# Attention: the second query chunk's probabilities are transposed by TensorE too, in a third filling of one PSUM bank

## The chip, the cores and the metric

The program runs on one core of one Trainium2 chip. The metric is the device time of one execution, in microseconds (us). Names of engines: PE is TensorE (PEld its weight loads), DVE is VectorE, ACT is ScalarE, POOL is GpSimd, and SP is the queue of SyncE, from which most DMAs are issued.

## The reference, cut to what matters

Causal attention over 4 batches and 12 heads of 448 tokens of 64 numbers, then two mixture-of-experts layers with top-1 routing (1792 tokens, 768 numbers, 8 experts, 1024 hidden numbers). The change touches the attention alone.

```python
scores = scale * np.matmul(q, k.transpose(0, 1, 3, 2))
scores = np.where(mask, -1000000000.0, scores)      # mask: above the diagonal
scores = scores - np.max(scores, axis=-1, keepdims=True)
attn = np.exp(scores)
attn = attn / (np.sum(attn, axis=-1, keepdims=True) + 1e-09)
out = np.matmul(attn, v)
...
x = _moe_ref(x=x, **moe_kwargs)
return _moe2_ref(x=x, **moe2_kwargs)
```

## The kernel before

**Tiling.** Two heads make a pair (index e is 0 or 1), 24 pairs in all. The 448 queries of a head are 4 chunks of 112 (c is 0 to 3). Chunk c sees c + 1 blocks of 112 keys, so a head has 1 + 2 + 3 + 4 = 10 blocks of 112x112 probabilities. They lie in one tile `ex` in SBUF, chunk by chunk: `boff` (L392) gives the first block of each chunk, [0, 1, 3, 6].

**A loop of stages.** One pass of the loop over g works on four pairs at once: scores and exponentials of pair g, the transposed probabilities of t = g - 1, the product with the values of v = g - 2, and routing work for r = g - 3. Each engine runs its instructions in the order in which the program was written.

- `qk` (L395): PE writes the mask and the scores of two chunks for both heads into four PSUM banks. `rowmax` (L410): DVE finds each row's extreme. `expo` (L415): ACT writes the exponentials to `ex`. Chunks 0 and 1 come first, chunks 2 and 3 later in the pass; there are four banks, so the next scores wait for the exponentials before.
- The product with the values needs the probabilities with keys in the partitions, so each block is transposed, as a high half and a low half in f16. **By DMA:** chunks 0, 1 and 2 (ND = 6 blocks a head): `halves_hi` (L424) lets ACT write `ah`, one instruction a head, and `halves_lo` (L429) lets DVE write `al` = `ex` - `ah`, one a head; `transposed` (L420) issues a DMA transpose from SP for each, into `th` and `tl`. **By PE:** chunk 3 (4 blocks): `last_chunk` (L436) has PE transpose the four blocks of one head into the left 448 columns of one PSUM bank, `tb[0]`; ACT then writes the high half `ph`, and DVE the low half `pl`. This is one filling of the bank; there are two in a pass, one for each head (`late[0]` and `late[1]`).
- `values` (L449): for each block five small matmuls into `av` (and, for the last group of columns, into the right part of `tb[1]`, called the tail). `combine` (L479): DVE divides by the row sums and writes `xb`.
- `route_t` (L495): PE transposes 128 columns of `xb` into the left of `tb[1]`; ACT and DVE split them into `xTh` and `xTl`; `route_l` (L508) multiplies them with the router's weights.
- Once a batch is done, its routing (a few dozen tiny DVE instructions, some PE work, a few POOL instructions and DMAs) is spread over three passes: `tick` takes one step of it after many of the big DVE instructions. Its PE work writes the right part of `tb[0]` (`side`, L338), and only the step that `tick(True)` takes, right after the first `qk` of a pass, may start that PE work.
- `scale_pair` and `split_v` on POOL prepare later pairs.

**SP in a pass:** DMA transposes of `ah` from the pass before, loads for four pairs ahead, DMA transposes of `al`, stores of `xb`. From pass 18 on, one weight load too.

After the attention the two expert layers follow, on PE almost without a gap.

Of the kernel before, what the change touches and what calls it, by code (L numbers as in the profile page):

```python
# [9 lines left out]
F32 = mybir.dt.float32  # L10
F32R = mybir.dt.float32r
BF16 = mybir.dt.bfloat16
F16 = mybir.dt.float16
# [43 lines left out]
def attention_two_moe_kernel(  # L57
# [243 lines left out]
    def drain(gen):  # L301
        for _ in gen:
            pass
# [12 lines left out]
    NB = NCH * (NCH + 1) // 2  # L316
    ND = NB - NCH
    exs = [at_p.tile([CP, 2, NB, CP], F32, name=f"ex{i}") for i in range(NEX)]
# [4 lines left out]
    phs = [av_p.tile([CP, 2 * NCH * CP + 16], F16, name=f"ph{i}") for i in range(NTP)]  # L323
    pls = [av_p.tile([CP, 2 * NCH * CP + 16], F16, name=f"pl{i}") for i in range(NTP)]
    for t in ahs + als:
        vec.memset(t[:, :, :, CP:], 0.0)
# [5 lines left out]
    for t in phs + pls:  # L332
        vec.memset(t[:, 2 * NCH * CP :], 0.0)


    tb = [ps_t.tile([P, 512], F32, tag="t", name="tb0"), ps_x.tile([P, 512], F32, tag="t2", name="tb1")]

    def side():  # L338

        return tb[0][:, S:] if tb else ps_t.tile([P, 512], F32, tag="t", name="t")  # L340

# [49 lines left out]

    boff = [0, 1, 3, 6]  # L392
    scs, nms, avs = {}, {}, {}
# [30 lines left out]
    def halves_hi(g):  # L424
        for e in range(2):
            act.activation(ahs[g % NAH][:, e, :, :CP], exs[g % NEX][:, e, :ND], AF.Copy, scale=ASC)
            transposed(ths[g % NTH], ahs[g % NAH], e)
# [7 lines left out]

    def last_chunk(g, e):  # L436

        pt = tb[0][:CP, :S]
        for j in range(NCH):
            pe.transpose(pt[:, j * CP : (j + 1) * CP], exs[g % NEX][:, e, ND + j], ident[:CP, :CP])  # L440
        yield
        ph, pl = (t[g % NTP][:, e * S : (e + 1) * S] for t in (phs, pls))
        act.activation(ph, pt, AF.Copy, scale=ASC)
        yield
        vec.scalar_tensor_tensor(out=pl, in0=pt, scalar=ASC, in1=ph, op0=ALU.mult, op1=ALU.subtract)
        tick()

    VW = HD + 1

    def values(g, e):  # L450

        if e == 1 and g not in tails:
            tails[g] = tb[1][:, S:]
        if e == 0:
            avs[g] = ps_x.tile([P, 512], F32, tag="av", name=f"av{g}")
        v0, v1, v2 = (t[:, e] for t in vss[g])
        for c in range(NCH):
            k = c if e == 0 else NCH + (c - 1) % NCH
            at = k * VW
            for j in range(c + 1):  # L460
                if c < NCH - 1:
                    o = (e * ND + boff[c] + j) * CP
                    hi, lo = (t[g % NTH][:CP, o : o + P] for t in (ths, tls))
                else:
                    o = (e * NCH + j) * CP
                    hi, lo = (t[g % NTP][:, o : o + P] for t in (phs, pls))
# [316 lines left out]
    for g in range(NPR + 3):  # L783
# [12 lines left out]
        if 0 <= v < NPR and v % PB == 0:  # L796
            xbs[v // PB] = xb_p.tile([CP, NCH, D], F32, tag="xb", name=f"xb{v // PB}")
        late = [last_chunk(t, e) if 0 <= t < NPR else iter(()) for e in range(2)]
        if g < NPR:
            qk(g, (0, 1))  # L800
        tick(True)
        if g < NPR:
            for c in range(2):
                both(rowmax, g, c)
                if g == c == 0:
                    both(expo, 0, 0, ticks=False)
                    scale_pair(1, vec)
            for c in range(g == 0, 2):
                both(expo, g, c, ticks=False)
        next(late[0], None)  # L810
        next(late[0], None)
        if 0 <= t < NPR:
            halves_lo(t, (0,))
        next(late[0], None)
        if 0 <= t < NPR:
# [16 lines left out]
        if 0 <= v < NPR:  # L832
            values(v, 0)
        if PB <= r < NPR and r % PB < NCH:
# [8 lines left out]
        if g < NPR:  # L843
            qk(g, (2, 3))
            for c in range(2, NCH):
                both(rowmax, g, c)
        next(late[1], None)
        for c in range(2, NCH):
            if g < NPR:
                both(expo, g, c, ticks=False)  # L850
            next(late[1], None)
        if 0 <= v < NPR:
            values(v, 1)
        if 0 <= r < NPR:
            route_l(r)
        if 0 <= v < NPR:
            combine(v, xbs[v // PB])
        if g < NPR:
            halves_hi(g)
        if g + 2 < NPR:  # L860
            scale_pair(g + 2, pool)
        if g == 0:
# [656 lines left out]
```

## Time and profile before

| what | us |
|---|---|
| median of 3 runs | 905.91 (905.5 to 911.83) |
| the profiled execution | 908.99 |
| its span, first to last instruction | 907.3 |
| PE busy | 848.7 (94%) |
| DVE busy | 678.2 (75%) |
| ACT busy | 427.1 (47%) |
| POOL busy | 399.0 (44%) |

A busy time counts the time in which at least one instruction of the engine is on record. PE's matmuls overlap and their ends are modelled, so the starts of its instructions say more than their lengths. A wait "A <- B" is idle time of A that ended when B did; "issue" is idle time for which the profile shows no reason. The clock of PE is either 2.4 GHz (1.00 in the columns) or 1.2 GHz (0.50).

### The profile page before, as it was taken

The page shows a single profiled execution, that of the slowest core. Times are in us where ns is not written, and L with a number is a line of the kernel's source. Part 1 is how long each engine was busy: PE and PEld are TensorE (multiplying, and loading weights), DVE is VectorE, ACT ScalarE, POOL GpSimd, SP SyncE. Part 2 cuts the span into 40 slices and gives each one's busy share as a digit, 9 for nine tenths or more (in the row PEclk, how much of TensorE's full clock was granted, in tenths as well). Part 3 has the DMA queues.
Part 4 walks back from the last instruction along what each step waited for, and adds up shares of the span by engine and source line. Part 5 has one row for each costly group of instructions (what it writes and reads, how often), then busy time and mean ns, then how long its engine had stood idle before and what let it go on. Part 6 is the DMA issues. An engine that isn't in the chain of part 4 may idle for free. (4 is left out here: it accounts for less than half of the span.)

```text
span 907.3 us, 20634 instructions
## 1 busy us (share of the span) xinstructions
PE 848.7 (94%) x6818; PEld 729.4 (80%) x6818; DVE 678.2 (75%) x1782; ACT 427.1 (47%) x777; POOL 399.0 (44%) x433
## 2 busy tenths in 40 slices
PE   5999999988788999999999999999999999999985
PEld 2677776766576899988899989888898898998984
DVE  6888998987876766787747964468786778976783
ACT  4667867775435754575535552245112133221323
POOL 6224245423266264544542564432654544545530
PEclk8899999998799999999999999999999999999997
DMA  7799998998737774687515761120291133511110
GB/s 227 143 160 164 206 199 178 206 174 169 238 97 262 280 260 163 210 290 257 185 46 172 239 229 62 49 73 6 62 328 56 54 108 117 182 43 59 49 38 16
DMA packets 114451, 137.39 MB, mean 151 GB/s; under 512 B 78381, under 2 KB 82787, under 8 KB 114288
## 3 DMA queue, kind: packets, MB, share of 16 engines
q1 hardware_dynamic: 101376, 108.76, 44.4%
q0 software_dynamic: 12912, 26.83, 9.3%
q8 instruction: 57, 0.93, 0.4%
q14 instruction: 106, 0.87, 0.3%
HBM read 101.48 MB, written 19.92 MB: 134 GB/s over the span
## 5 line engine op out<-in xcount | busy, mean ns | idle before, releaser
L748 POOL DMA_INDIRECT xg<-x,xi x128 | 134.4, 1050 | 101.2 <-DMA x<-yb,mg 47.7
L956 PE MATMUL h<-w1h,xh 128*128 128x512 f32 x408 | 164.6, 403 | 2.4 <-issue 1.4
L958 PE MATMUL h<-w1h,xl 128*128 128x512 f32 x408 | 161.1, 395 | 0.9 <-DVE xl L941 0.9
L957 PE MATMUL h<-w1l,xh 128*128 128x512 f32 x408 | 161.2, 395 | 0.7 <-DVE w1l L698 0.7
L1021 PE MATMUL o<-w2h,hh 128*128 128x384 f32 x528 | 137.5, 341 | 0.2 <-issue 0.2
L1021 PE MATMUL o<-w2h,hl 128*128 128x384 f32 x528 | 135.3, 337 | 0.5 <-DVE hl L971 0.5
L1021 PE MATMUL o<-w2l,hh 128*128 128x384 f32 x528 | 134.4, 336 | 0.0
L998 DVE STREAM_TRANSPOSE hs<-h 32x256 f32<-32x256 f32 x240 | 107.1, 446 | 14.3 <-PE h L958 8.5
L418 ACT ACTIVATE ex<-sc,nm 112x112 f32<-112x112 f32 (+1 forms) x192 | 82.8, 499 | 60.9 <-DVE nm L413 58.6
L1021 PEld LDWEIGHTS o<-w2h,hl 128*128 128x128 f32 x528 | 95.3, 188 | 0.8 <-DVE hl L971 0.8
L1021 PEld LDWEIGHTS o<-w2h,hh 128*128 128x128 f32 x528 | 94.0, 188 | 1.8 <-issue 0.4
L1021 PEld LDWEIGHTS o<-w2l,hh 128*128 128x128 f32 x528 | 95.2, 188 | 0.1
L1004 ACT ACTIVATE hh<-hs 128x512 fp32r<-128x512 f32 x30 | 18.4, 631 | 157.7 <-PE o L1021 86.5
L958 PEld LDWEIGHTS h<-w1h,xl 128*128 128x128 f32 x408 | 77.0, 189 | 19.3 <-DVE xl L941 1.6
L956 PEld LDWEIGHTS h<-w1h,xh 128*128 128x128 f32 x408 | 77.2, 189 | 18.8 <-issue 2.3
L957 PEld LDWEIGHTS h<-w1l,xh 128*128 128x128 f32 x408 | 77.3, 189 | 17.9 <-DVE w1l L698 2.6
L413 DVE TENSOR_REDUCE nm<-sc 112x1 f32<-112x112 f32 (+1 forms) x192 | 74.7, 438 | 19.0 <-PE sc L407 18.8
L698 DVE TENSOR_TENSOR w1l<-w1r,w1h 128x1024 fp32r<-128x1024 f32 x66 | 76.4, 1219 | 9.2 <-ACT w1h L696 5.8
L698 DVE TENSOR_TENSOR w2l<-w2r,w2h 128x768 fp32r<-128x768 f32 x78 | 68.8, 951 | 8.6 <-ACT w2h L696 5.6
L407 PE MATMUL sc<-r 64*112 64x112 f32 (+3 forms) x384 | 64.5, 458 | 3.9 <-DVE rt_ren L175 3.9
L696 ACT CAST w1h<-w1r 128x1024 fp32r<-128x1024 f32 x64 | 62.4, 1047 | 9.2 <-PE h L958 5.2
L929 DVE STREAM_TRANSPOSE xr<-xg 128x768 f32<-128x768 f32 x31 | 50.3, 1623 | 17.7 <-DMA xg<-x,xi 11.1
(316 smaller groups left out, 1735.6 us busy)
## 6 DMA issues: line engine op xcount, KB each, us to landing
w1r<-in_w1a SPq DMA_DIRECT2D x48, 512.0 KB
w2r<-in_w2a SPq DMA_DIRECT2D x64, 384.0 KB
r<-in_kqP SPq DMA_DIRECT2D x24, 448.0 KB
w1r<-in_w1b SPq DMA_DIRECT2D x18, 512.0 KB
w2r<-in_w2b SPq DMA_DIRECT2D x24, 384.0 KB
vr<-in_vh SPq DMA_DIRECT2D x24, 224.0 KB
x<-xb SPq DMA_DIRECT2D x16, 336.0 KB
xg<-x,xi POOLq DMA_INDIRECT x128
```

What stands on the lines that cost most here:

```text
L407: pe.matmul(scs[2 * g + e, c][:CP, :n], lhsT=r[rs, 1, c * CP : n], rhs=r[rs, 0, :n], start=False, stop=True, skip_group_check=True)
L413: vec.tensor_reduce(out=nms[h][:, c : c + 1], in_=scs[h, c][:CP, : CP * (c + 1)], axis=AX.X, op=ALU.min)
L418: act.activation(dst, scs.pop((h, c))[:CP, :n], AF.Exp, bias=nms[h][:, c : c + 1], scale=-1.0)
L696: act.copy(hi[k], r[k])
L698: vec.tensor_sub(lo[k], r[k], hi[k].bitcast(F32))
L748: pool.indirect_dma_start(out=xgs[j % 3][:, q * (D // Q) : (q + 1) * (D // Q)], out_offset=None, in_=quarters, in_offset=IND(ap=xi[:, q : ...
L929: vec.transpose(xr.rearrange("p k (q r) -> p q k r", q=Q), xgs[j % 3].rearrange("p (q r k) -> p q k r", q=Q, k=KD))
L956: pe.matmul(hps, lhsT=xh[:, c], rhs=w1h[c][:, ns], start=(c == 0), stop=False)
L957: pe.matmul(hps, lhsT=xh[:, c], rhs=w1l[c][:, ns], start=False, stop=False)
L958: pe.matmul(hps, lhsT=xl[:, c], rhs=w1h[c][:, ns], start=False, stop=(c == KD - 1))
L998: vec.transpose(hr[cols, :, rows], hps[rows, q * 256 : (q + 1) * 256].rearrange("p (c k) -> p k c", c=QR))
L1021: pe.matmul(ops[:, n, :384], lhsT=h[f // KH][:, f % KH], rhs=w[f][:, n * 384 : (n + 1) * 384], start=(f == 0 and st == 0), stop=(f == KF - ...
```

## The change

It alters which blocks go by DMA and in which order the work of a pass is written.

- Chunk 1's two blocks of each head (four for a pair) leave the DMA transposes: ND is 4 blocks a head in place of 6, and `boff` is [0, 4, 1, 6], so that chunks 0 and 2 lie side by side.
- `last_chunk` becomes `turned_part` with three parts: part 0 and 1 are the four blocks of chunk 3 of either head, as before; part 2 is the two blocks of chunk 1 of both heads, into the new tiles `qh` and `ql`.
- `halves_hi`: the first head's `ah` stays on ACT, the second head's goes to POOL. `scale_pair` is written ahead of it.
- Order: the first filling stands between the exponentials of chunk 0 and of chunk 1; the second stands behind the products of chunks 0, 2 and 3 of the first head and ahead of the second `qk`; the third stands behind the second `qk` and the first head's chunk 1. `tick(True)` moves behind the second `qk`.
- `side` is the right part of `tb[1]` in place of `tb[0]`. The second head's products are taken in the order 1, 2, 3, 0, so that the tail is written last.

```diff
     NB = NCH * (NCH + 1) // 2
-    ND = NB - NCH
+    ND = NCH
...
-        return tb[0][:, S:] if tb else ps_t.tile([P, 512], F32, tag="t", name="t")
+        return tb[1][:, S:] if tb else ps_t.tile([P, 512], F32, tag="t", name="t")
...
-    boff = [0, 1, 3, 6]
+    boff = [0, 4, 1, 6]
...
     def halves_hi(g):
         for e in range(2):
-            act.activation(ahs[g % NAH][:, e, :, :CP], exs[g % NEX][:, e, :ND], AF.Copy, scale=ASC)
+            ah, ex = ahs[g % NAH][:, e, :, :CP], exs[g % NEX][:, e, :ND]
+            if e == 0:
+                act.activation(ah, ex, AF.Copy, scale=ASC)
+            else:
+                pool.tensor_scalar(out=ah, in0=ex, scalar1=ASC, scalar2=1.0, op0=ALU.mult, op1=ALU.mult)
             transposed(ths[g % NTH], ahs[g % NAH], e)
...
-    def last_chunk(g, e):
+    def turned_part(g, part):
 
         pt = tb[0][:CP, :S]
-        for j in range(NCH):
-            pe.transpose(pt[:, j * CP : (j + 1) * CP], exs[g % NEX][:, e, ND + j], ident[:CP, :CP])
-        yield
-        ph, pl = (t[g % NTP][:, e * S : (e + 1) * S] for t in (phs, pls))
+        blocks = [(part, boff[3] + j) for j in range(NCH)] if part < 2 else [(e, boff[1] + j) for e in range(2) for j in range(2)]
+        for k, (e, j) in enumerate(blocks):
+            pe.transpose(pt[:, k * CP : (k + 1) * CP], exs[g % NEX][:, e, j], ident[:CP, :CP])
+        yield
+        at = part * S if part < 2 else 0
+        ph, pl = (t[g % NTP][:, at : at + S] for t in ((phs, pls) if part < 2 else (qhs, qls)))
         act.activation(ph, pt, AF.Copy, scale=ASC)
         yield
         vec.scalar_tensor_tensor(out=pl, in0=pt, scalar=ASC, in1=ph, op0=ALU.mult, op1=ALU.subtract)
         tick()
+        yield
...
-        late = [last_chunk(t, e) if 0 <= t < NPR else iter(()) for e in range(2)]
+        parts = [turned_part(t, k) if 0 <= t < NPR else iter(()) for k in range(3)]
         if g < NPR:
             qk(g, (0, 1))
-        tick(True)
...
-            for c in range(g == 0, 2):
-                both(expo, g, c, ticks=False)
-        next(late[0], None)
-        next(late[0], None)
+            if g:
+                both(expo, g, 0, ticks=False)
+        next(parts[0], None)
+        next(parts[0], None)
+        if g < NPR:
+            both(expo, g, 1, ticks=False)
...
         if 0 <= v < NPR:
-            values(v, 0)
+            values(v, 0, (0, 2, 3))
+        if v >= 0:
+            drain(parts[1])
...
             qk(g, (2, 3))
+        tick(True)
+        drain(parts[1])
+        if 0 <= v < NPR:
+            values(v, 0, (1,))
+        next(parts[2], None)
...
         if 0 <= v < NPR:
-            values(v, 1)
+            values(v, 1, (1, 2, 3, 0))
...
+        if g + 2 < NPR:
+            scale_pair(g + 2, pool)
         if g < NPR:
             halves_hi(g)
-        if g + 2 < NPR:
-            scale_pair(g + 2, pool)
```

**PE, in the pass g = 10, at the second `qk`.** Rows name instructions as the profile does, without the small numbers of tiles where they don't matter. Before, the four masks (L401) and the scores of chunks 2 and 3 (L407) follow the last products of the first head (L473), and the second filling (L440) stands behind them:

```order
L473 MATMUL av_2028<-r_235,pl_229 128x65
L401 LDWEIGHTS identb
L401 MATMUL sc_2_2082<-mask,identb 128x112
...
L407 MATMUL sc_2_2082<-r_1220 112x336
L407 MATMUL sc_2_2084<-r_1220 112x336
L407 MATMUL sc_3_2086<-r_1220 112x448
L407 MATMUL sc_3_2088<-r_1220 112x448
L440 MATMUL tb_253<-ident,ex_216 112x112 x4
L476 LDWEIGHTS th_223
```

With the change the second filling (L449 now) stands ahead of the masks (L405), and behind the scores come ten products from the new tiles `qh` and `ql`, then the third filling:

```order
L484 MATMUL av_2090<-r_239,pl_229 128x65
L449 MATMUL tb_261<-ident,ex_216 112x112 x4
L405 LDWEIGHTS identb
L405 MATMUL sc_2_2140<-mask,identb 128x112
...
L411 MATMUL sc_3_2146<-r_1258 112x448
L484 LDWEIGHTS qh_231
L484 MATMUL av_2090<-r_239,qh_231 128x65
...
L484 MATMUL av_2090<-r_239,ql_233 128x65
L449 MATMUL tb_261<-ident,ex_216 112x112 x4
L484 LDWEIGHTS qh_231
```

So the second filling moved ahead of four score matmuls, and a pass has three fillings of `tb[0]` where it had two.

**DVE, in the same pass.** Before, from the second pair of row extremes to the combine of the pass:

```order
L413 TENSOR_REDUCE nm_2002<-sc_1_1994 112x1
L431 SCALAR_TENSOR_TENSOR al_220<-ex_216,ah_218 112x6x112
L445 SCALAR_TENSOR_TENSOR pl_230<-tb_253,ph_228 112x448
L431 SCALAR_TENSOR_TENSOR al_220<-ex_216,ah_218 112x6x112
L505 TENSOR_TENSOR xTl_2025<-tb_254,xTh_2024 128x448
L413 TENSOR_REDUCE nm_2000<-sc_2_2082 112x1
...
L413 TENSOR_REDUCE nm_2002<-sc_3_2088 112x1
L445 SCALAR_TENSOR_TENSOR pl_230<-tb_253,ph_228 112x448
L484 TENSOR_SCALAR rinv_2162<-av_2028 112x8
```

With the change:

```order
L417 TENSOR_REDUCE nm_2064<-sc_1_2056 112x1
L439 SCALAR_TENSOR_TENSOR al_220<-ex_216,ah_218 112x4x112
L455 SCALAR_TENSOR_TENSOR pl_230<-tb_261,ph_228 112x448
L439 SCALAR_TENSOR_TENSOR al_220<-ex_216,ah_218 112x4x112
L516 TENSOR_TENSOR xTl_2087<-tb_262,xTh_2086 128x448
L455 SCALAR_TENSOR_TENSOR pl_230<-tb_261,ph_228 112x448
L417 TENSOR_REDUCE nm_2062<-sc_2_2140 112x1
...
L417 TENSOR_REDUCE nm_2064<-sc_3_2146 112x1
L455 SCALAR_TENSOR_TENSOR ql_234<-tb_261,qh_232 112x448
L495 TENSOR_SCALAR rinv_2230<-av_2090 112x8
```

The two `al` are 448 columns wide in place of 672, the second `pl` moved ahead of the row extremes of chunks 2 and 3, and `ql` is new in its old place.

## Rows read from the trace of the kernel before

**Rows 1.** Stretches: us; PE, PEld, DVE, ACT, POOL busy; PEclk, DMA share, GB/s.

```profile
34.23:220.70 186.47, 172.37 (x2958) 131.65 (x2954) 163.13 (x447) 134.85 (x303) 73.80 (x85) 0.96 0.96 181
245.00:907.30 662.30, 636.46 (x3401) 571.21 (x3401) 472.47 (x1164) 261.74 (x416) 304.46 (x302) 0.99 0.40 137
```

**Rows 2.** PE in order of time, one undisturbed pass: start, length, instruction.

```profile
85.77 0.37 PE L401 MATMUL sc<-mask,identb 112*128 112x112 bf16 x4
...
86.83 0.59 PE L440 MATMUL tb<-ident,ex 112*112 112x112 f32 x4
87.26 0.55 PE L501 MATMUL tb<-ident,xb 112*128 112x112 f32 x4
87.64 0.19 PE L473 MATMUL av<-r,th 112*128 112x65 bf16 x1
...
89.32 0.36 PE L401 MATMUL sc<-mask,identb 112*128 112x112 bf16 x4
...
93.14 0.37 PE L513 MATMUL lg<-xTh,enT 128*16 128x448 f32 x1
...
93.56 0.27 PE L401 MATMUL sc<-mask,identb 112*128 112x112 bf16 x2
```

**Rows 3.** DVE in order of time, the same pass.

```profile
85.56 0.17 DVE L484 TENSOR_SCALAR rinv<-av 112x8 f32<-112x8 f32 x1 [0.20 <-PE av L473]
...
86.73 1.04 DVE L413 TENSOR_REDUCE nm<-sc 112x1 f32<-112x112 f32 x4
87.69 0.84 DVE L431 SCALAR_TENSOR_TENSOR al<-ex,ah 112x672 f16<-112x672 f32 x1
89.39 0.62 DVE L445 SCALAR_TENSOR_TENSOR pl<-tb,ph 112x448 f16<-112x448 f32 x1 [0.85 <-ACT ph L443]
89.93 0.85 DVE L431 SCALAR_TENSOR_TENSOR al<-ex,ah 112x672 f16<-112x672 f32 x1
90.69 0.62 DVE L505 TENSOR_TENSOR xTl<-tb,xTh 128x448 fp32r<-128x448 f32 x1
91.23 1.97 DVE L413 TENSOR_REDUCE nm<-sc 112x1 f32<-112x336 f32 x4
```

**Rows 4.** DVE in order of time: the first combine, and the one 21 passes on.

```profile
34.23 0.17 DVE L484 TENSOR_SCALAR rinv<-av 112x8 f32<-112x8 f32 x1 [0.28 <-PE sc L401]
...
220.70 0.16 DVE L484 TENSOR_SCALAR rinv<-av 112x8 f32<-112x8 f32 x1
```

**Rows 5.** Waits from 34.23 to 220.70 us: who, for whom, us, times, longest.

```profile
PEld L473 <- DMA tl<-al: 8.5, 9, 1.8
...
PEld L473 <- issue: 3.1, 5, 0.7
...
PE tb L440 <- DVE r1lgr L591: 1.4, 2, 0.7
...
PE tb L440 <- DVE cnt L622: 1.1, 2, 0.5
```

**Rows 6.** Busy time by stretch where PEclk is under 1.00.

```profile
150.00:160.00 10.00, 10.00 (x146) 7.29 (x148) 7.23 (x18) 6.83 (x15) 5.47 (x7) 0.83 0.77 180
180.00:190.00 10.00, 8.16 (x115) 6.32 (x116) 6.97 (x25) 4.62 (x12) 1.98 (x3) 0.83 0.98 206
200.00:220.00 20.00, 17.75 (x260) 13.08 (x260) 14.46 (x41) 12.51 (x29) 12.34 (x16) 0.83 0.98 191
```

**Rows 7.** PE's weight loads in order of time: the last waits ahead of those stretches.

```profile
148.30 0.11 PEld L473 LDWEIGHTS <-tl 112*128 112x128 f16 x2 [1.21 <-DMA tl<-al]
...
183.90 0.11 PEld L473 LDWEIGHTS <-tl 112*128 112x128 f16 x2 [1.29 <-DMA tl<-al]
```

**Rows 8.** SP's queue in order of time, in the pass of rows 2.

```profile
87.17 2.54 SPq L421 DMA_TRANSPOSE th<-ah  x2
...
91.99 2.54 SPq L421 DMA_TRANSPOSE tl<-al  x2
```

**Rows 9.** POOL in order of time: a copy with a factor, beside `al`.

```profile
87.73 1.23 POOL L381 TENSOR_SCALAR r<-r 128x448 f32<-128x448 f32 x1
```

More of the change, by code (lines that the diff above doesn't have):

```diff
@@ L324, in attention_two_moe_kernel @@
     pls = [av_p.tile([CP, 2 * NCH * CP + 16], F16, name=f"pl{i}") for i in range(NTP)]
+    qhs = [av_p.tile([CP, S + 16], F16, name=f"qh{i}") for i in range(NTP)]
+    qls = [av_p.tile([CP, S + 16], F16, name=f"ql{i}") for i in range(NTP)]
     for t in ahs + als:
@@ L333, in attention_two_moe_kernel @@
         vec.memset(t[:, 2 * NCH * CP :], 0.0)
+    for t in qhs + qls:
+        vec.memset(t[:, S:], 0.0)
     tb = [ps_t.tile([P, 512], F32, tag="t", name="tb0"), ps_x.tile([P, 512], F32, tag="t2", name="tb1")]
     def side():
-        return tb[0][:, S:] if tb else ps_t.tile([P, 512], F32, tag="t", name="t")
+        return tb[1][:, S:] if tb else ps_t.tile([P, 512], F32, tag="t", name="t")
     def prep_en():
@@ L446, in last_chunk, with values @@
         tick()
+        yield
     VW = HD + 1
-    def values(g, e):
+    def values(g, e, cs):
         if e == 1 and g not in tails:
             tails[g] = tb[1][:, S:]
-        if e == 0:
+        if g not in avs:
             avs[g] = ps_x.tile([P, 512], F32, tag="av", name=f"av{g}")
         v0, v1, v2 = (t[:, e] for t in vss[g])
-        for c in range(NCH):
+        for c in cs:
             k = c if e == 0 else NCH + (c - 1) % NCH
@@ L460, in values @@
             for j in range(c + 1):
-                if c < NCH - 1:
+                if c in (0, 2):
                     o = (e * ND + boff[c] + j) * CP
@@ L464, in values @@
                 else:
-                    o = (e * NCH + j) * CP
-                    hi, lo = (t[g % NTP][:, o : o + P] for t in (phs, pls))
+                    o = (e * (c + 1) + j) * CP
+                    hi, lo = (t[g % NTP][:, o : o + P] for t in ((phs, pls) if c == NCH - 1 else (qhs, qls)))
                 ops = ((hi, v1), (hi, v0), (hi, v2), (lo, v0), (lo, v1))
@@ L797, in attention_two_moe_kernel @@
             xbs[v // PB] = xb_p.tile([CP, NCH, D], F32, tag="xb", name=f"xb{v // PB}")
-        late = [last_chunk(t, e) if 0 <= t < NPR else iter(()) for e in range(2)]
+        parts = [turned_part(t, k) if 0 <= t < NPR else iter(()) for k in range(3)]
         if g < NPR:
             qk(g, (0, 1))
-        tick(True)
-        if g < NPR:
             for c in range(2):
@@ L807, in attention_two_moe_kernel @@
                     scale_pair(1, vec)
-            for c in range(g == 0, 2):
-                both(expo, g, c, ticks=False)
-        next(late[0], None)
-        next(late[0], None)
+            if g:
[4 more added lines that the diff above has]
+            both(expo, g, 1, ticks=False)
         if 0 <= t < NPR:
             halves_lo(t, (0,))
-        next(late[0], None)
+        next(parts[0], None)
         if 0 <= t < NPR:
@@ L844, in attention_two_moe_kernel @@
             qk(g, (2, 3))
+        tick(True)
[3 more added lines that the diff above has]
+        next(parts[2], None)
+        if g < NPR:
             for c in range(2, NCH):
                 both(rowmax, g, c)
[L847 to L851, printed above, removed]
+            both(expo, g, 2, ticks=False)
+        next(parts[2], None)
+        if g < NPR:
+            both(expo, g, 3, ticks=False)
+        next(parts[2], None)
         if 0 <= v < NPR:
-            values(v, 1)
+            values(v, 1, (1, 2, 3, 0))
         if 0 <= r < NPR:
```

## The prediction

> **What bounds the kernel now.** I read the stretches first. The experts, from 245 us on, keep PE busy 96% of the time, and the change does not touch them [rows 1]: what the attention gains or loses should reach the end nearly one to one. So the question is the length of the steady passes, 34.23 to 220.70 us.
>
> Then PE in order of time, in one pass without disturbance [rows 2]. From the first masks at 85.77 to those of the next pass at 93.56 no row has an idle time; each instruction starts where the one before leaves off. A pass is thus 7.79 us of pure PE work: masks and scores of chunks 0 and 1 take 1.06 (85.77 to 86.83), a filling of four transposes 0.43 (to 87.26), the transposes of `xb` 0.38 (to 87.64), fifty products 1.68 (to 89.32), the router's two products 0.42 (93.14 to 93.56).
>
> DVE in the same pass is nearly as full [rows 3]. Start to start: combine 1.17 (85.56 to 86.73), four row extremes 0.96, one `al` 0.76 (89.93 to 90.69), one `pl` 0.54 (89.39 to 89.93), `xTl` 0.54, four more extremes 1.97. With two `al` and two `pl` that is 1.17 + 0.96 + 1.52 + 1.08 + 0.54 + 1.97 = 7.24 us. ACT is busy 135 of 186 us and POOL 74 [rows 1]; neither bounds a pass.
>
> But 21 passes take 220.70 - 34.23 = 186.47 us [rows 4], 8.88 each. PE's work explains 21 x 7.79 = 163.6; 22.9 us are lost. The waits name most of it. PE's weight loads wait 8.5 us for the DMA transposes into `tl`, in nine places, 1.8 at most; 3.1 for nothing that the profile shows; and the first filling waits 1.4 + 1.1 = 2.5 for DVE to read the routing's numbers out of the same bank [rows 5]. And the granted clock: three stretches, 40 us together, have a mean PEclk of 0.83 [rows 6], so 0.17 x 2 x 40 = 13.6 us were at 1.2 GHz, which costs a bound PE up to half, 6.8. Together 8.5 + 3.1 + 2.5 + 6.8 = 20.9 of the 22.9. The last waits ahead of the first two slow stretches are both for `tl`, 1.2 and 1.3 us long [rows 7].
>
> **What the change costs.** A third filling: four more transposes, 0.43 us of a PE that has no gap, so 21 x 0.43 = 9.0 us. Three more fillings lie in the first two passes and the last one, where PE is not full; between nothing and 1.3, I take 0.4. On DVE the two `al` become as wide as `pl` (448), 0.54 in place of 0.76, and `ql` adds 0.54: 2 x (0.54 - 0.76) + 0.54 = +0.10, a pass of 7.34. That is below PE's new 7.79 + 0.43 = 8.22, so it costs nothing while PE bounds; without that cover it would be 21 x 0.10 = 2.1. ACT gives one `ah` to POOL, makes the other smaller and gains one `qh`: less than before, off the path.
>
> POOL's new `ah` is a copy with a factor of 448 columns; the nearest row is 1.23 us, taken beside an `al` [rows 9]. Its two waiters are the DMA transpose of the second head, which holds SP's queue, and the second `al` on DVE, behind which the rest of DVE's pass is queued. It needs only chunk 2's exponentials, which ACT writes ahead of chunk 3's, so POOL starts before ACT could have. `scale_pair` stands ahead of it now and waits for loads four passes old: no cost. Only in a pass in which POOL has routing DMAs first can it be late.
>
> The order: the second filling now stands ahead of the second `qk`, and needs `tb[0]` back from the first `pl`. I lay the two ways side by side, from the last product of a pass. PE: 0.42 (router) + 1.06 + 0.43 + 0.38 + 40 of 50 products, 1.34 = 3.63. DVE: 0.20 until the combine starts [rows 3], 1.17, 0.96, one narrow `al` 0.54, then `pl` of 0.62 = 3.49. DVE is ahead by 0.14 only. ACT's first `ph` has to come in time for that; it does, since it moved ahead of chunk 1's exponentials, where before `pl` waited 0.85 for it [rows 3]. A margin so thin will be missed sometimes: between nothing and 0.3 a pass, I take 0.1, 2.1 us. Where routing steps are mixed into DVE's chain it will surely be missed. A wait of the routing kind now is 0.7 and 0.5 long [rows 5]; about six passes have such steps, so 0 to 4.2; I take 2.5. The third filling needs the second `pl`, which lies before DVE's 1.97 of row extremes, while PE does a whole `qk` in between: no wait.
>
> **What the change gives.** First, `tl`. SP issues two `th` and two `tl` of 672 columns, 1.27 each, 5.08 us of a pass [rows 8]. The last issue ends at 94.53; the next pass's products come 1.87 after its start, at 95.43 [rows 2]. That is 0.9 us for a transfer, and so PE waits in some passes. Now a transpose has 448 columns: its issue takes between 1.27 (a fixed price) and two thirds of it; the four end 0 to 1.7 sooner, and the use is 0.43 later in a longer pass. With 0.43 alone nine waits of 0.94 on the mean would keep 4.6 of 8.5 us; with 2.1 none is left. DMA engines are also 96% taken now [rows 1], a third of the transposed columns leaves them, and the last `ah` no longer stands behind the first on one engine. I take 1.0 left: -7.5.
>
> Second, the clock: two of the three slow stretches follow `tl` waits and should go with them, -4.5; the third, past 200 us, follows none (183.90 is the last of the nine) and may stay or not. I take 1.7 left of 6.8: -5.1. Third, those unexplained waits, which I take to be helped by emptier DMA engines: between 0 and -3.1, I take -1.6. Fourth, routing leaves `tb[0]`: -2.5.
>
> **Sum:** 9.0 + 0.4 + 2.1 + 2.5 - 7.5 - 5.1 - 1.6 - 2.5 = -2.7 us. The profiled execution took 908.99, its span 907.3; by its own time it would be 906.3. The median of the runs is 905.91, 3.1 lower, and I set the difference against that: 903.2.
>
> **Rivals.**
> *A, everything lost comes back.* The waits for `tl`, the slow stretches, the routing wait and the unexplained ones all vanish, and DVE's chain keeps its 0.14: 9.0 - 8.5 - 6.8 - 2.5 - 3.1 = -11.9, less some 2 that always remain: about 896. For it: only two of the nine waits for `tl` are followed by a slow stretch [rows 5, 7], so an even fuller PE may hold the clock throughout. Against it: routing's DVE steps stay.
>
> *B, slower: the ring through `tb[0]`.* Three fillings share one bank, so each waits for DVE's reading of the one before, and DVE's reading waits for ACT. The place is the second filling, the margin 0.14. If the chain is 0.6 longer than I lay it out (a late combine, `ah` late from POOL, semaphores at each of five hand-overs), each pass loses 0.46 more, 21 x 0.46 = 9.7: 913. It decides from about 0.27 over the chain of 3.49 on, where it eats the 2.7. For it: five hand-overs that rows 3 show only in another order. Against it: a late DVE is late for `combine` too, and the pass before has 0.9 us to spare on DVE.
>
> *C, slower: transposes do not hold the clock.* PE at 1.2 GHz costs half of each slow stretch, 13.6 / 3 / 2 = 2.3 us. Two more such stretches than before undo the gain; four give about 912. For it: waits of 1.2 us were enough twice [rows 7]. Against it: a pass already has 0.43 + 0.38 + 0.43 of transposes in 7.79 [rows 2], and the mean PEclk over the 21 passes is 0.96 [rows 1], nearly all of the loss in the three stretches [rows 6]. The Trainium skill says (TensorE: Matmul & The Clock Gate, Part 4: PE-mode transpose) that a transpose does not count as busy for the clock in the way that other matmuls do; by it a pass with 1.67 us of transposes in 8.22 is worse off than one with 1.24 in 7.79, which no run here shows yet.
>
> *D, nothing moves:* the third filling's 9.0 and the waits removed cancel to within 3 us; this is part of my forecast, which is itself a small difference of large terms.
>
> **How the numbers follow.** The forecast with D (898 to 908) gets 0.5; A 0.22; B 0.2; C 0.08. The predicted time is 903.2. The range leaves out half of A's lower side and a part of B and C: 892 to 914. About 1%, 9.1 us, is what a measurement of this kernel can tell from no change: faster than 896.8 takes more than half of A and a little of the forecast, 0.18; slower than 915.0 takes the far ends of B and C, 0.12; the rest is 0.70.
>
> **What would show it.** Right: undisturbed passes of 8.2 us where they were 7.8; no PE wait for `tl`; PEclk of 1.00 from 35 us on but for one stretch; transposes on SP well under 1.27 each. The wait to look for is PE on `tb` for DVE's `pl` at the second filling: under 0.2 a pass in my forecast, 0.5 in B. Wrong: DVE waiting for POOL's `ah` in every pass; undisturbed passes of 7.8, which would mean that PE had room that I did not see; or waits for `tl` as large as before.

## The result: 0.5% slower, and where the time went

The changed kernel takes 912.18 us (median of 15 runs) against 907.45 for the kernel before, run beside it: a ratio of 1.0051, 95% interval 1.0031 to 1.0072. The range held the time; the forecast of -2.7 us did not come true, it became +4.7. The profiled execution took 911.23, its span is 909.4.

The stretches after, with the 21 passes between the first and the 22nd combine in the first line (columns as in [rows 1]):

```profile
39.61:220.94 181.33, 174.10 (x3046) 136.51 (x3043) 167.78 (x473) 130.87 (x304) 79.11 (x107) 1.00 0.79 159
245.00:909.40 664.40, 637.81 (x3409) 572.01 (x3409) 473.88 (x1170) 263.56 (x419) 310.41 (x305) 0.99 0.40 137
```

The passes took 181.33 us where [rows 1] has 186.47, and the granted clock is at 2.4 GHz throughout them. The difference goes with the clock: two profiles with the passes of before that also stay at 2.4 GHz have 180.50 and 180.56 us (below). And the passes begin 5.4 us later, as DVE's first combine shows beside [rows 4]:

```profile
39.61 0.17 DVE L495 TENSOR_SCALAR rinv<-av 112x8 f32<-112x8 f32 x1 [0.37 <-PE sc L405]
...
220.94 0.15 DVE L495 TENSOR_SCALAR rinv<-av 112x8 f32<-112x8 f32 x1
```

Where the start lost them is seen at the row extremes of chunk 2 in pass 1. DVE before, and then DVE after, with PE's two fillings after:

```profile
21.79 0.91 DVE L413 TENSOR_REDUCE nm<-sc 112x1 f32<-112x336 f32 x2
```

```profile
18.56 0.45 DVE L417 TENSOR_REDUCE nm<-sc 112x1 f32<-112x112 f32 x2 [1.71 <-PE sc L411]
...
26.18 0.62 DVE L455 SCALAR_TENSOR_TENSOR pl<-tb,ph 112x448 f16<-112x448 f32 x1 [4.12 <-ACT ph L453]
26.72 1.97 DVE L417 TENSOR_REDUCE nm<-sc 112x1 f32<-112x336 f32 x4
28.69 0.62 DVE L455 SCALAR_TENSOR_TENSOR ql<-tb,qh 112x448 f16<-112x448 f32 x1
```

```profile
24.58 0.98 PE L449 MATMUL tb<-ident,ex 112*112 112x112 f32 x4
26.86 0.60 PE L449 MATMUL tb<-ident,ex 112*112 112x112 f32 x4 [1.29 <-DVE pl L455]
```

In pass 1 there are no values yet, so nothing lies on PE between the scores and the second filling. DVE stands 4.12 us at that filling's `pl`, and the row extremes queued behind it start 4.9 us later than before.

The other end is POOL's order. POOL and ACT where attention meets the experts, before and then after:

```profile
211.33 1.10 POOL L729 DMA_INDIRECT mg<-meta,ld_idxm  x1 [0.18 <-issue]
214.02 0.95 POOL L732 DMA_INDIRECT xg<-x,mg  x1 [1.58 <-DMA mg<-meta,ld_idxm]
236.55 0.95 POOL L642 DMA_INDIRECT meta<-mt,r1sir  x1 [21.47 <-DVE ld_rowm L286]
...
241.53 1.20 POOL L170 TENSOR_TENSOR rt_sr<-r1ss,half 112x4 f32<-112x4 f32 x1
...
242.62 1.06 ACT L940 CAST xh<-xt 128x384 fp32r<-128x384 f32 x2 [1.88 <-PE xt L938]
```

```profile
230.91 1.06 POOL L653 DMA_INDIRECT meta<-mt,r1sir  x1 [10.52 <-DVE ld_rowm L286]
...
241.02 1.66 POOL L740 DMA_INDIRECT mg<-meta,ld_idxm  x1 [4.93 <-DMA meta<-mt,r1sir]
245.27 0.95 POOL L743 DMA_INDIRECT xg<-x,mg  x1 [2.59 <-DMA mg<-meta,ld_idxm]
246.25 1.05 POOL L170 TENSOR_TENSOR rt_sr<-r1ss,half 112x4 f32<-112x4 f32 x1
...
250.15 0.48 ACT L959 CAST xh<-xt 128x384 fp32r<-128x384 f32 x1 [8.48 <-PE xt L957]
```

Before, the early gather of the first expert tile (`mg`, then `xg`) ran at 211 us, ahead of batch 2's four scatters into `meta`. The new order carries batch 2's routing further within pass 24, so that its scatters are issued ahead of the gather, which stands at that pass's end. Now the gather waits 4.93 us for the scatters to land and 2.59 for its own first half, the norm's power step (`rt_s`) behind it is held too, and ACT's `xh`, the first cast of the experts, waits 8.48 us for the tile.

A table of the marks, means over three profiles of the kernel before (the prediction's and two more, below) and two of the changed one:

| us | before | changed | difference |
|---|---|---|---|
| first combine | 34.23, 34.87, 32.90 | 39.61, 38.53 | +5.1 |
| 21 passes | 186.47, 180.50, 185.12 | 181.33, 183.07 | -1.8 |
| last two passes | 14.02, 17.54, 14.03 | 16.53, 16.06 | +1.1 |
| last combine to first cast of the experts | 7.90, 7.62, 8.16 | 12.68, 11.88 | +4.4 |
| span | 907.3, 906.8, 906.2 | 909.4, 913.2 | +4.5 |

The four parts make +8.8; some 4 us come back behind the cast. The row of the 21 passes mixes executions with and without stretches at 1.2 GHz.

### The profile page after: what moved, and what is told of

It reads as the page before. It is cut to its first block, busy times and chain, and to the rows that moved or that the text cites. A ratio compares the mean times of both kernels' runs of the same rounds, so it can differ in the third digit from the quotient of the medians.

```text
span 909.4 us, 20926 instructions
## 1 busy us (share of the span) xinstructions
PE 854.2 (94%) x6914; PEld 738.0 (81%) x6914; DVE 681.7 (75%) x1810; ACT 421.7 (46%) x777; POOL 411.2 (45%) x457
## 5 line engine op out<-in xcount | busy, mean ns | idle before, releaser
L759 POOL DMA_INDIRECT xg<-x,xi x128 | 137.2, 1072 | 102.4 <-DMA x<-yb,mg 55.0
L422 ACT ACTIVATE ex<-sc,nm 112x112 f32<-112x112 f32 (+1 forms) x192 | 85.4, 496 | 48.8 <-DVE nm L417 47.9
L411 PE MATMUL sc<-r 64*112 64x112 f32 (+3 forms) x384 | 62.4, 447 | 3.9 <-DVE rt_ren L175 3.9
```

The source lines that it names most:

```text
L411: pe.matmul(scs[2 * g + e, c][:CP, :n], lhsT=r[rs, 1, c * CP : n], rhs=r[rs, 0, :n], start=False, stop=True, skip_group_check=True)
L422: act.activation(dst, scs.pop((h, c))[:CP, :n], AF.Exp, bias=nms[h][:, c : c + 1], scale=-1.0)
L759: pool.indirect_dma_start(out=xgs[j % 3][:, q * (D // Q) : (q + 1) * (D // Q)], out_offset=None, in_=quarters, in_offset=IND(ap=xi[:, q : ...
```

## The experiments

Times are given as ratios to the kernel before, run on the same chip, with 95% intervals; a kernel without one was executed and profiled once.

**POOL's order.** gather_first:

```diff
         parts = [turned_part(t, k) ...]
+        if g == NPR:
+            m1.gather_early((0,), 2 * S)
...
-            m1.gather_early((0,), 2 * S)
             load_lead(m1, 2)
```

> The changed kernel with one thing moved: the early gather of the first MoE tile is issued on POOL at the beginning of pass 24 and not at its end, so that it stands ahead of batch 2's four scatters in POOL's order, as it does in before. Theory Q (queue order pays): in the changed kernel POOL's gather at 241.02 waits 4.93 us for the scatters and the one at 245.27 waits 2.59 for the first, the power step behind it starts at 246.25 (241.53 before) and the first cast of the MoE part at 250.15 (242.62 before). Without that the gap from the last combine to that cast falls from 12.7 to 7.9 us, the first scatter of results comes 3 to 4 us earlier, and the time falls by 2 to 3.5 us from 912.2 (1.5 us of any lead are lost later, as between the two profiles: 6.1 us at 276, 2.1 at the end). Rival W (the first block waits for something else, the split weights or the routing of batch 3): the gathers move and the cast does not, time within 1 us of 912.2.

It gave 1.0017 (0.9994 to 1.0039), 909.34 us. POOL and ACT:

```profile
220.67 1.11 POOL L740 DMA_INDIRECT mg<-meta,ld_idxm  x1 [0.16 <-issue]
223.51 0.96 POOL L743 DMA_INDIRECT xg<-x,mg  x1 [1.73 <-DMA mg<-meta,ld_idxm]
230.26 0.95 POOL L653 DMA_INDIRECT meta<-mt,r1sir  x1 [5.67 <-DVE ld_rowm L286]
...
239.51 1.04 POOL L170 TENSOR_TENSOR rt_sr<-r1ss,half 112x4 f32<-112x4 f32 x1 [4.07 <-ACT xTh L515]
...
243.00 0.88 ACT L960 CAST xh<-xt 128x384 fp32r<-128x384 f32 x2 [1.99 <-PE xt L958]
```

The cast comes 6.2 us after the last combine (236.82) instead of 12.7, and the time is 2.8 us below the changed kernel's 912.18 (0.34% by the two ratios): theory Q, with a shorter gap than its 7.9. The other way round, before_gather_late puts only this order into the kernel before:

```diff
-            m1.gather_early((0,), 2 * S)
...
         if g == NPR + 2:
+            m1.gather_early((0,), 2 * S)
             warm(ps_T, "T", WV)
```

> The kernel before with one thing moved: the early gather of the first MoE tile is issued in pass 26, behind batch 2's four scatters on POOL, as the changed kernel has it. Nothing of the change itself is in it. Theory Q (the order on POOL alone makes the loss at the end of attention): before scatters at 236.55 to 241.5; the gather behind them waits as in the changed kernel (4.9 us, then 2.6, then 4.9 from the second gather to the cast), so the first cast of the MoE part goes from 242.6 to 253 to 257, and the time rises from 907.9 by 6 to 12 us less what is given back later, to 912 to 919. Rival N (the loss is the changed kernel's own, through its fillings at the end): the cast moves by less than 2 us, the time by less than 1.5.

It gave 1.0117 (1.0089 to 1.0145), some 9 to 11 us:

```profile
241.67 0.99 POOL L729 DMA_INDIRECT mg<-meta,ld_idxm  x1 [5.28 <-DMA meta<-mt,r1sir]
244.18 0.96 POOL L732 DMA_INDIRECT xg<-x,mg  x1 [1.52 <-DMA mg<-meta,ld_idxm]
245.16 1.05 POOL L170 TENSOR_TENSOR rt_sr<-r1ss,half 112x4 f32<-112x4 f32 x1
...
249.12 1.06 ACT L940 CAST xh<-xt 128x384 fp32r<-128x384 f32 x2 [13.69 <-PE xt L938]
```

The waits are of the size of the changed kernel's; the cast came earlier than I expected because attention itself was done sooner (last combine 229.63, so 19.5 us to the cast). The order alone makes a loss; nothing else of the change is in this kernel. How large the loss is in the changed kernel, gather_first tells.

**The start.** old_start gives passes 0 to 2 the order of before:

```diff
+            if g < 3:
+                tick(True)
...
-        if v >= 0:
+        if g >= max(3, 2):
             drain(parts[1])
...
+            next(parts[1] if g < 3 else iter(()), None)
             both(expo, g, 2, ticks=False)
...
+        if g < 3:
+            drain(parts[1])
+            drain(parts[2])
```

(with both `ah` on ACT in those passes, and chunk 1's exponentials ahead of the first filling).

> The changed kernel with the first three passes (0, 1 and 2) in the order of before: routing step after the first score products, second and third filling behind the row extremes of chunks 2 and 3, both 448-wide upper halves on ACT. From pass 3 on it is the changed kernel. Theory S (the start pays): the first combine, 34.23 us before and 39.61 after, comes back to 34.2 to 35.0, the last combine (237.47 after) comes at 232 to 233, and the time falls by 4 to 5.4 us from 912.2, to 907 to 908: as before. Rival P (the start is only shifted work: what the steady passes gained belongs to it, so that they take back what the start gives): the first combine comes back, the 21 passes rise from 181.3 towards 186.5, and the time stays within 1.5 us of 912.2.

It gave 1.0047 (1.0022 to 1.0072), 911.99 us; the first combine came at 37.38 only. With the gather moved as well:

> Both edits: the first three passes in the order of before, and the early gather ahead of batch 2's scatters. Theories S and Q together: the parts add, 912.2 - 4.7 - 2.7 = 904.8, between 903 and 906.5, that is below before (907.45) by 1 to 4.5 us, about what the steady passes gained. Rival P with Q: 909 to 911. Rival P with W: within 1.5 us of 912.2.

0.9990 (0.9963 to 1.0017), 905.31 us, 4.0 less than gather_first by the medians and 2.5 by the ratios; first combine at 35.86. So the start seemed to be worth 2.5 to 4 us in one case and nothing in the other, and 1.6 to 3.1 us of it were still missing. Three kernels, each with one edit to gather_first and executed once, first the fillings of passes 1 and 2 behind the row extremes:

> The kernel gather_first with the second and third filling of passes 1 and 2 behind the row extremes of chunks 2 and 3 as before, but the routing step and POOL's share left as the change has them. It divides what the start lost (first combine 34.23 before, 39.35 in gather_first, 35.9 to 37.4 with the whole old order). Theory F (the fillings' place): the row extremes of chunk 2 in pass 1, 26.72 after and 21.79 before, come 2 to 3 us earlier, the first combine at 36.5 to 37.5. Rival T (the routing step and the rest of the order): both move by less than 1 us, and the old order's gain is the step's.

The row extremes of chunk 2 in pass 1 came at 23.32, 3.4 us earlier than in the changed kernel, but the first combine at 38.14, only 1.2 earlier than in gather_first: neither theory's number. The third filling, now the last thing of the pass, took the place of the second. In that kernel DVE shows it, twice:

```profile
26.21 0.62 DVE L455 SCALAR_TENSOR_TENSOR pl<-tb,ph 112x448 f16<-112x448 f32 x1 [0.24 <-ACT ph L453]
28.10 0.62 DVE L455 SCALAR_TENSOR_TENSOR ql<-tb,qh 112x448 f16<-112x448 f32 x1 [1.26 <-ACT qh L453]
...
35.25 0.62 DVE L455 SCALAR_TENSOR_TENSOR pl<-tb,ph 112x448 f16<-112x448 f32 x1 [0.17 <-ACT ph L453]
37.14 0.62 DVE L455 SCALAR_TENSOR_TENSOR ql<-tb,qh 112x448 f16<-112x448 f32 x1 [1.26 <-ACT qh L453]
```

From `pl` to the `ql` behind it through the one bank it is 1.89 us (26.21 to 28.10, 35.25 to 37.14), with nothing else on DVE.

> The kernel gather_first with the routing step of the first three passes back at its old place, ahead of the row extremes; fillings and POOL's share as the change has them. First row extreme of pass 1: 18.56 us in the changed kernel, 16.57 before. If the step makes these 2 us: 16.6 to 17.2, and the first combine 1 to 2 us earlier than 39.35, at 37.4 to 38.4. If POOL's share or the order of the exponentials makes them: 18.3 to 18.7, first combine 39 or more.

First row extreme of pass 1 at 16.52, the 2.0 us in full; first combine at 38.62, 0.7 earlier, under the least that I expected.

> The kernel gather_first with the third filling of passes 1 and 2 in the routing bank, order as the change has it. If the one bank makes the early fillings wait (1.3 us for the second's lower half in pass 1): the third filling's lower half in pass 1, 28.69 us in the changed kernel, comes 0.5 to 1.5 us earlier, the first combine at 38 to 39. If the row extremes that are queued on DVE behind the second filling make the loss: no change over 0.4 us, first combine at 39 to 39.6.

`ql` came at 27.98 and the first combine at 38.85, both in the range of the bank. But the first row extreme of pass 1, which the bank cannot touch, was 0.46 early already (18.10), and `ql` still starts where DVE's row extremes end (26.01 + 1.97): in this order the bank does next to nothing. These first combines can't divide the 5 us: four profiles with the changed kernel's own start have 38.53 to 39.61, and the granted clock from 22 to 34 us differs, 0.50 in early_step, 1.00 in changed_again. No single piece brings the 5 us. All of them together, with a bank of its own for the second filling of pass 24 but without the moved gather, beside the changed kernel on the same chip:

```diff
-        pt = tb[0][:CP, :S]
+        if (g, part) == (NPR - 1, 1):
+            pt = ps_T.tile([P, 512], F32, tag="T", name="T1")[:CP, :S]
+        else:
+            pt = tb[part == 2 and g < 2][:CP, :S]
```

(here `g` is the pair whose blocks are turned; the order is that of old_start).

> The changed kernel, unchanged, timed again beside the next one and profiled again. Both theories: 911 to 913.5, 3.5 to 6 us over before; first combine 39 to 39.8; 21 passes 180.5 to 182.5 (six profiles of its passes so far: 180.99 to 182.24) with no stretch at 1.2 GHz between 45 and 215 us; first cast of the MoE part at 248 to 251. If instead its passes spread as those of before do (180.5 to 186.5), the clock is not steadier in it and nothing of the change's gain on the passes is shown.

> The changed kernel with the first three passes in the order of before and the two fillings in banks of their own, that is both_plus_banks without the moved gather: POOL's order stays that of the changed kernel. First combine at 34 to 34.5. Theory S (the start pays by itself): the last combine and the scatters behind it come 3 to 5 us earlier, the first cast at 245 to 247, the time 3 to 5 us below changed_again. Rival P (what the start gains is taken back, by the passes or ahead of POOL's gather): the first combine comes back, the time stays within 1.5 us of changed_again.

changed_again gave 1.0061 (1.0041 to 1.0081), start_and_banks 1.0004 (0.9984 to 1.0024): 5.6 us apart by the medians, 5.2 by the ratios. Their first combines and casts:

```profile
38.53 0.17 DVE L495 TENSOR_SCALAR rinv<-av 112x8 f32<-112x8 f32 x1 [0.38 <-PE sc L405]
...
249.54 0.48 ACT L959 CAST xh<-xt 128x384 fp32r<-128x384 f32 x1 [7.56 <-PE xt L957]
```

```profile
34.26 0.17 DVE L498 TENSOR_SCALAR rinv<-av 112x8 f32<-112x8 f32 x1 [0.40 <-PE sc L405]
...
243.71 0.48 ACT L975 CAST xh<-xt 128x384 fp32r<-128x384 f32 x1 [9.00 <-PE xt L973]
```

The start is back at 34.3, the cast 5.8 us earlier, and the time follows: theory S, by slightly more than it gave. old_start, 0.2 us below the changed kernel with its first combine 1.2 to 2.2 earlier, does not contradict it: its interval is 2.3 us wide to either side. ACT's 9.00 shows that POOL's order is still there. Taking both away:

> The kernel old_start_gather_first with two fillings in banks of their own: the third filling of passes 1 and 2 in the routing bank, which no routing uses yet, and the second of pass 24 in a bank that is free by then. Theories S, Q and E together: the 1.3 to 1.7 us wait for the pass's shared bank before the third filling goes in both early passes, first combine at 34 to 35 (35.9 in old_start_gather_first at the lower clock, 37.4 in old_start); pass 24 with the one behind it 15.5 (16.4); the time 902 to 904.5, below before by 3 to 6 us. Rival: the waits move to ACT and DVE, which the early passes then wait for: 905 to 906.5, as old_start_gather_first.

0.9970 (0.9944 to 0.9996), first combine at 34.12: 0.3% below before, the one kernel here whose interval ends below 1, and just so. I had expected 3 to 6 us; it is 2.7 by the ratio, 4.2 by the medians. Whether the banks add to old_start_gather_first these two intervals do not say.

**The end.** own_bank_at_end has only the bank for pass 24 out of the diff above.

> The changed kernel with the second filling of the last pair (pass 24, where no scores are left) in a bank of its own, so that neither it nor the third filling waits for the pass's shared bank. Theory E (the fillings' chain sets the last passes): pass 24 (9.43 us) falls by the 0.61 us wait of the third filling and what follows it to 8.5 or below, the time by 0.6 to 1.2 us. Rival C (the half clock, 1.2 GHz from 223.4 to 230.2 us in the profile after, is what lengthens pass 24): pass 24 stays at 9 or more wherever its clock is at the lower level, and comes to 7 to 7.8 where it is not; the time stays within 0.6 us of 912.2.

1.0049 (1.0022 to 1.0077). Pass 24 fell to 6.86 us, but the next rose to 8.64 (7.1 after); together 15.5 against 16.5, and nothing of it arrives. The unchanged kernel has nearly the same in its second profile, 7.39 and 8.67 (changed_again), so the fall is no sign of the bank. It names no cause.

**The passes.** Two more profiles of the kernel before:

> The kernel before, unchanged, profiled again. The 21 passes between the first and the 22nd combine took 186.47 us in the profile that the prediction rests on, and 180.56 in before_gather_late, whose passes are those of before, with the same waits for the transfer of tl (8.5 us) but no stretch at 1.2 GHz. Theory L (the three slow-clock stretches of the prediction's profile, 5.1 us of its sum, were one execution's, not the kernel's): here the passes come to 180 to 183 with one such stretch or none. Rival K (they belong to the kernel, the one in before_gather_late is the exception): 185 to 188, two or three stretches between 100 and 215 us.

> As before_second_look, a third profile of the same kernel, for the spread of the 21 passes: theory L 180 to 183, rival K 185 to 188. If the looks differ by more than 3 us among themselves, the clock's part of the prediction's sum is a matter of the execution, and only its mean can be counted.

The stretch of the 21 passes and the wait for `tl` in them, in before_second_look and then in before_third_look:

```profile
34.87:215.37 180.50, 165.79 (x2957) 127.77 (x2954) 164.18 (x447) 135.01 (x304) 75.17 (x85) 1.00 0.99 185
```

```profile
PEld L473 <- DMA tl<-al: 11.9, 11, 2.7
```

```profile
32.90:218.02 185.12, 170.62 (x2958) 130.56 (x2954) 165.97 (x448) 135.49 (x304) 73.65 (x85) 0.97 1.00 185
```

```profile
PEld L473 <- DMA tl<-al: 11.4, 11, 2.2
```

The second profile has longer waits for `tl` than the prediction's (11.9 against 8.5 us in [rows 5]) and yet 6 us less in its passes; its clock stayed at 2.4 GHz. The third has three stretches at 1.2 GHz again, at other places (55, 131 and 212 us). What the clock takes differs from one execution to the next, and was not more where the waits were longer. Neither L nor K alone: two of four profiles with the passes of before have such stretches (before_gather_late, 180.56, has none).

Nor is the changed kernel free of them. changed_again, which I expected to show none, has one near 188 us and a longer sum of passes than I gave:

```profile
38.53:221.60 183.07, 175.62 (x3046) 137.89 (x3043) 168.10 (x472) 130.66 (x304) 79.27 (x107) 0.99 0.77 158
```

It is the one of eleven profiles with the changed kernel's passes that has such a stretch. That suggests that the change makes them rarer; four profiles of the passes before are too few to show it. At 2.4 GHz throughout, the changed passes are no shorter than those of before: 181.33 against 180.50 and 180.56.

The filling's price, with its work left out of gather_first:

```diff
+        if part == 2:
+            yield
+            yield
+            tick()
+            yield
+            return
         pt = tb[0][:CP, :S]
```

> The kernel gather_first without the work of the third filling: no transposes, no ACT split and no DVE split of chunk 1 (its products run on zeros), everything else in place. It prices the filling. By the prediction's term, 0.43 us a pass: undisturbed pass 8.06 to 7.6, the 21 passes from 181.7 to 172.7. By the difference of the undisturbed passes of the two profiles, 0.27 (8.06 against 7.79 before): 7.8, and 176. If the filling hides behind other work altogether: 8.06, and 181.7. In the first passes, where nothing covers its chain from TensorE over ACT to DVE, the first combine comes 1.5 to 4 us earlier than 39.35.

Combines of its undisturbed passes, then of the changed kernel's:

```profile
88.16 0.17 DVE L501 TENSOR_SCALAR rinv<-av 112x8 f32<-112x8 f32 x1 [0.61 <-PE tb L494]
...
95.81 0.17 DVE L501 TENSOR_SCALAR rinv<-av 112x8 f32<-112x8 f32 x1 [0.60 <-PE tb L494]
```

```profile
89.56 0.17 DVE L495 TENSOR_SCALAR rinv<-av 112x8 f32<-112x8 f32 x1 [0.40 <-PE tb L488]
...
97.62 0.17 DVE L495 TENSOR_SCALAR rinv<-av 112x8 f32<-112x8 f32 x1 [0.38 <-PE tb L488]
```

7.65 against 8.06: 0.41 us, the prediction's 0.43. But the 21 passes, gather_first and then without the filling:

```profile
39.35:221.09 181.74, 173.98 (x3046) 136.41 (x3043) 167.85 (x472) 130.67 (x304) 79.52 (x107) 1.00 0.76 159
```

```profile
38.88:219.07 180.19, 167.13 (x2966) 128.44 (x2963) 158.79 (x451) 124.31 (x284) 80.59 (x107) 1.00 0.78 160
```

PE loses 6.9 us of work and the passes 1.55 us, in one profile of each (two of the changed kernel are 1.7 apart); PE's idle time rises from 7.8 to 13.1. Only eight of gather_first's 21 passes have the undisturbed length (8.04 to 8.09). What holds the others is not PE's work alone. The first combine came at 38.88, 0.5 us earlier (1.5 if counted from the first row extreme of pass 1, at 19.45 here and 18.38 in gather_first), at the lower end of the 1.5 to 4 at best: the added filling's own work is the smaller part of what the start lost.

> The kernel gather_first with the second head's 448-wide upper half back on ACT (0.58 us an issue) instead of POOL (0.56). Prediction's reading: ACT is not the bound (busy 131 of 182 us over the passes), the 21 passes stay at 181.7 within 1. Rival: the half on ACT stands ahead of the next pass's exponentials, 21 x 0.5 = 10 us more ACT work on the chain from row extremes to exponentials, 184 to 190.

21 passes of 184.49 us, 2.75 more than gather_first. But 2.54 of these lie in the first pass (11.23 against 8.69), in which a stretch at 1.2 GHz from 46.0 to 49.4 us falls; the other twenty are 0.2 us longer together. PE's waits for `pl` rose from 2.0 us to:

```profile
PE tb L449 <- DVE pl L455: 6.9, 7, 1.7
```

Those waits are what the rival forecast; its 184 to 190 is not shown, and the prediction's reading holds outside the first pass. The routing's products back in the fillings' bank (`side()` returns `tb[0]` again):

> The kernel gather_first with the routing's small products back in the fillings' bank, as before. By the prediction's terms (2.5 us saved on TensorE, 2.5 us lost in DVE's chain) nothing moves: 21 passes 181.7 within 1. If the bank alone pays: 184.2, and TensorE's waits of the fillings for the routing's DVE steps (2.5 us of them before) come back. If the routing passes (9.0 to 10.0 us against 8.06) are set by DVE's chain: no change at all.

182.24 us, half a microsecond more: nothing moves. The term of -2.5 for taking routing out of `tb[0]` is not there.

## Why the prediction was wrong

**Steps that held.** The filling's price (0.43, measured 0.41); the undisturbed pass came to 8.06 us and not 8.22, since without the filling it is 7.65, 0.14 below the 7.79 of before. The waits for `tl`, forecast to fall by 7.5 to 1.0, fell by 5 to 8 (to 3.6 from 8.5, 11.9 and 11.4). Waits of the changed kernel from 39.61 to 220.94 us:

```profile
PEld L484 <- DMA tl<-al: 3.6, 6, 0.8
...
PE tb L449 <- DVE pl L455: 2.0, 4, 0.8
```

Rival B did not come. That the ring through `tb[0]` cost 2.0 where 2.1 was taken is chance: the four waits lie in the first of the 21 passes and in three with routing steps (at 43.59, 126.35, 136.11 and 145.11 us), and none in an undisturbed pass. So 1.2 us of them belong to the term for the routing passes (2.5), and nothing to the 2.1.

Rival C did not come either: PEclk is 1.00 and 0.99 over the passes of two profiles with a third more transposes. By the rule of the Trainium skill that the prediction weighed (TensorE: Matmul & The Clock Gate, Part 4: PE-mode transpose) the larger share of transposes would count against the clock; the traces do not show it for this mix.

**Steps that failed.** First, "So the question is the length of the steady passes", and for all that lies outside them: "Three more fillings lie in the first two passes and the last one, where PE is not full; between nothing and 1.3, I take 0.4." PE's free time was the wrong measure, and the new order was laid out for a steady pass only; what it does where no values lie between the fillings stood at nothing. There DVE stands 4.12 us at the second filling, a chain over PE, ACT and DVE, with the row extremes queued behind it, and the moved routing step puts 2.0 us more ahead of pass 1's row extremes (early_step). The work of the third filling alone is 0.5 to 1.5 us of it (no_third_filling). The start cost 5.1 us in the first combine and 5.2 to 5.6 in the time (start_and_banks); how this divides between the order, the step and the bank is not shown.

Second, "the change does not touch them", of the experts. The new order moved batch 2's scatters past the early gather on POOL, some 3 us here (gather_first) and 10 in the kernel before (before_gather_late). This stood in the order of POOL's instructions before any run; the prediction read the order only inside a pass. The Trainium skill says of these engines that their queues are strict FIFO (PSUM — Partial Sum Buffer, Engine vs sequencer instructions), so that one waiting instruction holds all behind it, and the trace agrees: the power step, which needs nothing of the gather, started 0.03 us after the gather's 0.95 us were over.

Third, "21 x 0.43 = 9.0" and, of DVE, "it costs nothing while PE bounds". Without the filling's work the passes were 1.55 us shorter and not 9.0 (no_third_filling), since PE bounds only some of them. In the seven passes with routing steps (the 11th to 13th, 17th to 19th and 21st of the changed kernel, 8.3 to 10.0 us) DVE is idle for 0.1 to 0.6 us and PE for 0.2 to 1.1; in six of them DVE is the fuller engine. One routing step of 112x32 numbers has grown there, DVE before and then POOL and DVE after:

```profile
129.38 0.24 DVE L595 SCALAR_TENSOR_TENSOR r1lgr<-r1lgr,tau_r,r1nrr 112x32 f32<-112x32 f32 x1
```

```profile
218.30 2.05 POOL L160 TENSOR_SCALAR w1h<-w1r 128x1024 fp32r<-128x1024 f32 x2
218.35 2.04 DVE L606 SCALAR_TENSOR_TENSOR r1lgr<-r1lgr,tau_r,r1nrr 112x32 f32<-112x32 f32 x1
```

In the three passes that have it, it takes 1.03, 1.03 and 2.04 us where it took 0.24, each time beginning 0.05 us behind a POOL instruction and ending with it; in halves_on_act, where POOL has no `ah` and comes to other work at other times, it takes 0.24 again. So a row that shows DVE busy can hold a wait. What these 3.4 us cost the kernel no run shows.

The counterpart, the clock's -5.1, was one execution's: the passes of before took 180.5 to 186.5 us. Without it the prediction's terms for the passes give +2.0, and at 2.4 GHz throughout +0.8 was measured; with it they give -3.1, beside -5.1 by the two first profiles. That these two lie near each other is luck: the prediction's profile had the clock's stretches and the first one after had none. The unexplained waits (-1.6) are missing in two of the three profiles of before as well; the changed kernel has 10.6 us of them on PE's weight loads, where PE itself shows none.

Fourth, a small one: the transposes on SP were to fall "well under 1.27 each". SP after, in an undisturbed pass, beside [rows 8]:

```profile
98.73 2.55 SPq L425 DMA_TRANSPOSE th<-ah  x2
...
103.29 2.50 SPq L425 DMA_TRANSPOSE tl<-al  x2
```

1.25 to 1.28 each, with a third fewer columns.

**What stays open.** What sets each of the passes that PE does not, beyond DVE's fullness in those with routing steps. Why some 4 us of the 8.8 come back behind the cast. And what pass 24's third filling costs: own_bank_at_end does not tell.

## What to carry to other kernels

Compare the order of instructions on every queue over the whole program, its two ends and the DMA-issuing engines too, and look for an instruction that has moved past one that it does not need: a reordering inside a loop also moves steps across the loop's end. Lay a new order out for a loop's first passes too, as a bare chain over all its engines, and do not price it by the free time of one. And multiply a price by the number of passes only after counting in how many of them that engine is the bound; a loss by the clock that one profile shows is to be seen in a second one before it enters a sum, and passes are compared at the same granted clock.

## What the runs showed of the hardware

The issue of a DMA transpose on SP took nearly the same for two widths: 1.27 us for 672 columns [rows 8], 1.25 to 1.28 for 448; over all 96 of a run the medians are 1.24 and 1.23 before, 1.21 after. POOL's copy with a factor of 448 columns takes 0.56 us for `ah` in the changed kernel. The 1.23 of [rows 9] is not that shape's price: the same instruction (L381) has a median of 0.57 over the 22 of the kernel before, and its 1.23 stood beside an `al` on DVE. That DVE and POOL hold each other up at such places is what these rows and those of `r1lgr` suggest; no experiment separates it.

```profile
96.23 0.56 POOL L434 TENSOR_SCALAR ah<-ex 112x448 f16<-112x448 f32 x1 [4.87 <-ACT ex L422]
```
